# Softmax of six attention units on ScalarE, regrouped dilated units, weights decoded in two parts, and a new written order in a fused attention and two-layer MLP kernel

## The chip, the cores and the metric

The kernel runs on one core of a Trainium2 chip. Its engines are TensorE (PE, matrix products), VectorE (DVE), ScalarE (ACT), GpSimd (POOL) and SyncE (SP, which here only issues DMAs). The metric is the time of one execution on the device in microseconds (us), as the median of several runs.

## The reference

Three stages run one after the other, all in fp32.

```python
# 1 attention: q, k, v are 2 x 8 x 576 x 64
rel = pos[:, None] - pos[None, :]
mask_plain = (rel >= 0) & (rel < 32)                       # heads 0-3
mask_dil = (rel >= 0) & (rel < 128) & (rel % 4 == 0)       # heads 4-7
scores = where(mask, q @ k.T / 8, -1e9)
x = softmax(scores) @ v                  # rearranged to 1152 tokens x 512
# 2 a SoLU layer: w_in 512 x 1024, w_out 1024 x 512 (both fp64 in HBM here)
h = x @ w_in;  solu = h * softmax(h)
x = ((solu - mean) / sqrt(var + 1e-6) * g_ln) @ w_out
# 3 four experts, weighted: w1 4 x 512 x 1024, w2 4 x 1024 x 512
out = sum_e p[:, e] * (relu(x @ w1[e]) @ w2[e])
```

## The kernel before, in words

**Precision.** Every large product is made of three fp32r products: each operand is split into a rounded high part and the rest (`xhi`, `xlo`, `whi`, `wlo`), and high x high, high x low and low x high are added in PSUM. `w_in` and `w_out` come as 64-bit floats and are decoded by `convert` (L182): ACT turns the low word into a number (L186) and takes the absolute value of the high word (L188), DVE shifts it (L190) and puts the sign back (L192), and DVE or POOL adds the low part (L194). Then `conv_in` rounds the result to `whi` (L219) and subtracts to get `wlo` (L221).

**Attention** (`att_U`, L253) is done in twelve units: for each of two batches three plain units (P.0 to P.2, four heads each, 192 positions) and three dilated ones (D.0 to D.2, each four heads, two residues at a time, 96 positions of one dilated sequence of 288). A unit is a mask product and 24 QK products (L262, L271), a row maximum (L279), a subtraction (L281) and a sum (L286) on DVE, one exponential on ACT (L284), a reciprocal, a scaling (L290), a transposition on PE (L309) or by DVE and a trip through HBM (the units in `ASWAP`, L295 to L303), the product with v (AV, L320), and the split into `xhi`, `xlo`. A PSUM tile for attention comes from a pool of two. v of a plain unit comes from a pool of two buffers (`vp`, L152).

**SoLU layer.** `moe_H(t)` (L344) makes 24 products (L350) for one tile of 128 tokens, six for each of four blocks of 128 rows of `w_in`; blocks 0 and 1 take the plain heads, 2 and 3 the dilated heads. Then come maximum (L355), exponential (L357), product with h (L359) and normalisation (L362 on ACT or L364 on DVE). `moe_T` (L369) transposes the tile, for tiles 3 to 8 through HBM (`swap_T`, L391). `moe_X(c, dp)` (L421) is the product with `w_out` for a chunk of three tiles, 48 products (L432), copied out at L435.

**Experts.** `up` (L548) and `down` (L601) run from about 150 us on, with products at L545 and L617. Steps of groups g = 1 to 7 are set by loops at the end of the kernel.

**What sets the order.** Up to the first expert group the order is a list written by hand (`ORDER`, L28): each name stands for one step of a generator, up to its next `yield`, for a load (`lP`, `lD`, `lI`, `lO`, `lvp`, `lvd`) or for warm-up products on a dummy tile (`F.n`, L84). A `+` after a name sets `alt`, which gives that step's copies to DVE rather than ACT and its additions to POOL rather than DVE. Each engine, and SP for all loads, runs its instructions in that order.

Of the kernel before, what the change touches and what calls it, by code (L numbers as in the profile page):

```python
# [8 lines left out]
F32 = mybir.dt.float32  # L9
BF16 = mybir.dt.bfloat16  # L10
# [43 lines left out]
def fused_kernel(ctx, tc, qkp, qkd, vp, vd, w_in, w_out, gp, w1, w2, out):  # L54
# [50 lines left out]
    ap2 = at.enter_context(tc.tile_pool(name="ap2", bufs=2))  # L105
    early = ExitStack()
# [3 lines left out]
    for b, p in enumerate((erp, ap1)):  # L110
        qkP.append([p.tile([128, 832], F32, name=f"qkP{b}{t}", tag=f"qkP{b}{t}") for t in range(3)])
        qkD.append([p.tile([128, 896], F32, name=f"qkD{b}{t}", tag=f"qkD{b}{t}") for t in range(3)])
        vdt.append([p.tile([128, 3, 4, D], F32, name=f"vd{b}{c}", tag=f"vd{b}{c}") for c in range(3)])
# [25 lines left out]
    for r in range(1, 4):  # L139
        nc.vector.tensor_copy(mask[32 * r:32 * r + 32, 2], m0[:, 2])  # L140
# [203 lines left out]
    def moe_H(t):  # L344
        pm = psm.tile([128, 2, 512], F32, name="pm", tag="pm")
        cols = slice(128 * t, 128 * t + 128)
        for n_, kk in enumerate(KORD):
# [4 lines left out]
            if n_ % HCUT[t] == HCUT[t] - 1:  # L352
                yield
# [433 lines left out]
```

## Time and profile before

| | us |
|---|---|
| median of 3 runs (lowest, highest) | 529.58 (528.38, 531.33) |
| profiled execution, first to last instruction | 528.5 |
| PE busy | 515.0 |
| DVE busy | 356.9 |
| ACT busy | 191.7 |
| POOL busy | 187.3 |

The profile gives for each engine its busy time; a matmul counts as busy while it waits in the pipeline, so the start times of matmuls say more than their durations. Its views are a table of stretches (busy time of each engine, granted clock of PE as a share of 2.4 GHz, share and rate of the DMAs), a timeline of instructions with what ended the idle time before them, and the chain of waits, followed back from the last instruction. The span is 528.5 us and lies inside the range of the timed runs.

### The profile page before, as it was taken

Reading aid. Unit: us, or ns where it says so; the run is one execution under the profiler, and the core shown is the slowest. Engines: PE = TensorE matmul, PEld = TensorE weight load, DVE = VectorE, ACT = ScalarE, POOL = GpSimd, SP = SyncE. Lnnn points to the kernel's source line nnn. Section 1 sums busy time; section 2 is a strip of 40 time slices with the busy share of each in tenths; the row PEclk is TensorE's granted clock in tenths of the full one; section 3 lists DMA queues with packets and bytes.
Section 4 is the critical chain, followed back from the end, with each engine's and each line's share of the span. In section 5 each row is a group of like instructions: output and inputs, shape, how many; then the busy total and the mean of one; then the engine's idle time right before and its main releaser. Section 6 shows DMA issues by size and latency. Waiting matters only on the chain.

```text
span 528.5 us, 9419 instructions
## 1 busy us (share of the span) xinstructions
PE 515.0 (97%) x3971; PEld 459.0 (87%) x3971; DVE 356.9 (68%) x474; ACT 191.7 (36%) x295; POOL 187.3 (35%) x130
## 2 busy tenths in 40 slices
PE   7799999999999999999999999999999999999997
PEld 3578898888999998998989899898989889898986
DVE  6889996777978874854685485568448656853632
ACT  3768965423254432321422232142214213312210
POOL 2554220312233532730571173048117313820300
PEclk9799999999999999999999999999999999999999
DMA  8966752448043001300400040040004002000022
GB/s 311 364 239 211 242 175 97 112 141 211 16 159 141 19 2 35 126 1 1 159 1 1 0 160 0 1 141 20 2 0 161 1 0 81 0 1 1 1 81 99
DMA packets 24490, 46.44 MB, mean 88 GB/s; under 512 B 4480, under 2 KB 9088, under 8 KB 24064
## 3 DMA queue, kind: packets, MB, share of 16 engines
q1 hardware_dynamic: 24448, 45.84, 25.6%
q8 instruction: 31, 0.51, 0.4%
q14 instruction: 11, 0.09, 0.0%
HBM read 39.34 MB, written 6.49 MB: 87 GB/s over the span
## 4 chain that ended last, share of the span: by engine, by line
PE 87%; DMA 7%; DVE 4%; ACT 1%; SPq 1%; issue 0%; DVEq 0%; ACTq 0%
PE pa L617 19%; PE pm L617 18%; PE pm L545 17%; PE pa L545 17%; PE pm L350 7%; PE pm L432 6%; DMA vp<-in_vp_dram 2%; PE pa L320 2%; DMA et<-dt 2%; DMA draw<-in_moe_w_in_dram 1%; DMA dt<-st 1%; PE pa L271 1%; DVE e L359 1%; DVE e L364 1%; PE pa L381 1%; DVE st L397 0%
## 5 line engine op out<-in xcount | busy, mean ns | idle before, releaser
L558 DVE SCALAR_TENSOR_TENSOR hl<-ct,hh 128x512 fp32r<-128x512 f32 (+1 forms) x64 | 63.6, 1012 | 35.3 <-ACT hh L556 35.3
L556 ACT ACTIVATE hh<-ct 128x512 fp32r<-128x512 f32 (+1 forms) x64 | 42.1, 682 | 48.7 <-DVE ct L588 20.7
L617 PE MATMUL pa<-wl,hh 128*128 128x512 f32 (+1 forms) x148 | 57.3, 387 | 0.0
L617 PE MATMUL pa<-wh,hh 128*128 128x512 f32 (+1 forms) x148 | 57.3, 387 | 0.0
L617 PE MATMUL pa<-wh,hl 128*128 128x512 f32 (+1 forms) x148 | 57.1, 386 | 0.0
L545 PE MATMUL pm<-xoh,hl 128*128 128x256 f32 (+1 forms) x192 | 56.8, 296 | 0.0
L545 PE MATMUL pa<-xoh,hl 128*128 128x256 f32 (+1 forms) x192 | 56.8, 296 | 0.0
L545 PE MATMUL pm<-xol,hh 128*128 128x256 f32 (+1 forms) x192 | 56.8, 296 | 0.0
L545 PE MATMUL pa<-xol,hh 128*128 128x256 f32 (+1 forms) x192 | 56.8, 296 | 0.0
L545 PE MATMUL pm<-xoh,hh 128*128 128x256 f32 (+1 forms) x192 | 56.8, 296 | 0.0
L545 PE MATMUL pa<-xoh,hh 128*128 128x256 f32 (+1 forms) x192 | 56.8, 296 | 0.0
L617 PE MATMUL pm<-wl,hh 128*128 128x512 f32 (+1 forms) x144 | 55.7, 387 | 0.0
L617 PE MATMUL pm<-wh,hh 128*128 128x512 f32 (+1 forms) x144 | 55.7, 387 | 0.0
L617 PE MATMUL pm<-wh,hl 128*128 128x512 f32 (+1 forms) x144 | 55.6, 386 | 0.0
L464 POOL TENSOR_TENSOR wl<-wl,wh 128x1024 fp32r<-128x1024 f32 x7 | 16.9, 2414 | 95.3 <-ACT wh L172 95.3
L622 DVE SCALAR_TENSOR_TENSOR xf<-pm,pr,xf 128x512 f32<-128x512 f32 (+1 forms) x32 | 23.6, 738 | 31.1 <-PE pm L617 31.1
L464 POOL TENSOR_TENSOR hl<-sw,hh 128x512 fp32r<-128x512 f32 x22 | 33.5, 1522 | 30.3 <-ACT hh L172 27.6
L622 DVE SCALAR_TENSOR_TENSOR xf<-pa,pr,xf 128x512 f32<-128x512 f32 (+1 forms) x32 | 23.6, 738 | 30.3 <-PE pa L617 30.3
L172 ACT CAST wh<-wl 128x1024 fp32r<-128x1024 f32 x16 | 16.8, 1052 | 71.0 <-PE pa L617 40.5
L572 POOL TENSOR_TENSOR ct<-ct,ct 128x512 f32<-128x512 f32 (+1 forms) x15 | 21.4, 1426 | 48.1 <-ACT ct L570 42.9
L545 PEld LDWEIGHTS pm<-xoh,hh 128*128 128x128 f32 x192 | 36.4, 190 | 0.3
L545 PEld LDWEIGHTS pm<-xol,hh 128*128 128x128 f32 x192 | 36.4, 190 | 0.3
(199 smaller groups left out, 1258.9 us busy)
## 6 DMA issues: line engine op xcount, KB each, us to landing
wl<-in_moe_w_dram SPq DMA_DIRECT2D x16, 512.0 KB, 3.7
cvr<-in_moe_w_out_dram SPq DMA_DIRECT2D x8, 512.0 KB, 3.6
rw<-in_moe_w_dram SPq DMA_DIRECT2D x8, 512.0 KB, 6.0
wh<-in_moe_w_dram SPq DMA_DIRECT2D x8, 512.0 KB
draw<-in_moe_w_in_dram SPq DMA_DIRECT2D x3, 1024.0 KB, 12.8
qkD<-in_qkd_dram SPq DMA_DIRECT2D x6, 448.0 KB, 6.4
dt<-st SPq DMA_DIRECT2D x5, 512.0 KB, 3.3
et<-dt SPq DMA_DIRECT2D x10, 256.0 KB, 4.2
```

The lines of the kernel that those rows point to most:

```text
L172: nc.scalar.copy(out, in_)
L271: nc.tensor.matmul(ps[32 * g:32 * g + 32, j, 64 * m:64 * m + 64], lhsT=qt[rows, h, xq:xq + 32], rhs=kt[rows, h, xq:xq + 64], start=False, ...
L320: nc.tensor.matmul(po[64 * (g % 2):64 * (g % 2) + 64, j, o:o + 32], lhsT=vt[rows, m, g, :], rhs=pt[rows, m, g, :], start=True, stop=True)
L350: nc.tensor.matmul(pm[:, n, :], lhsT=xx[:, kk, cols], rhs=ww["in", kk][:, 512 * n:512 * n + 512], start=(n_ == 0 and i < 2), stop=(n_ == K ...
L432: nc.tensor.matmul(pm[:, dd, 0:CW], lhsT=w_, rhs=x_[:, f, :], start=(f == 0 and i == 0), stop=(f == KF - 1 and i == 2))
L464: pick().tensor_tensor(out=out, in0=a, in1=b, op=op)
L545: nc.tensor.matmul(ps[:, ff, 0:n], lhsT=a[:, kk, fc], rhs=b[:, kk, :], start=kk == 0 and m == 0, stop=kk == 1 and m == 2)
L556: nc.scalar.activation(out=hv, in_=src, func=AF.Relu)
L558: nc.vector.scalar_tensor_tensor(out=lv, in0=src, scalar=0.0, in1=hv.bitcast(F32), op0=ALU.max, op1=ALU.subtract)
L572: poolv().tensor_tensor(out=c12, in0=c21, in1=c22, op=ALU.add)
L617: nc.tensor.matmul(po[:, 0, 0:dn], lhsT=h_[:, f, cols], rhs=w_, start=(f == 0 and i == 0), stop=(f == 3 and i == 2))
L622: nc.vector.scalar_tensor_tensor(out=acc[:, t, dc], in0=po[:, 0, 0:dn], scalar=pr[:, t, e:e + 1], in1=acc[:, t, dc], op0=ALU.mult, op1=ALU ...
```

## The change

1. In the six units of batch 1 (`EXPB`), ACT makes the subtraction and the sum with the exponential: one small copy scales the six negated maxima, then six exponentials of 64 columns each read the scores from PSUM with that maximum as their bias and write the sum through the accumulator. DVE keeps the maximum and adds 1e-9 to the sums.
2. A dilated unit holds other blocks of 32 positions (`DBLK`): unit 0 has positions 0, 128 and 160, unit 1 has 32, 64 and 192, unit 2 has 224, 256 and 96. Tile 0 of the SoLU layer then needs dilated unit 0 alone. The host lays out q, k and v accordingly, and a `qkd` load is 128x1024 in place of 128x896. The write of `xhi`, `xlo` of a dilated unit has up to three pieces in place of one or two.
3. `w_in` is decoded in two parts: `conv_high` makes `whi` from the high word alone, `conv_low` adds the low word and makes `wlo`, later. They have three buffers (`evas`) in place of two.
4. Tiles 0 and 1 (`FINE`) do the products with `whi` of blocks 0 and 1 first, then those with `wlo`, then the same for blocks 2 and 3.
5. v of the plain units has three buffers; masks are three in place of four; the program is built with `dynamic_dma_scratch_size=2048`.
6. `ORDER` is new throughout, up to the first expert group.

```diff
+EXPB = ("UD.0.1","UD.1.1","UD.2.1","UP.0.1","UP.1.1","UP.2.1")
+FINE = (0, 1)
+DBLK = ((0, 128, 160), (32, 64, 192), (224, 256, 96))
 ORDER = """
-lP.0.0+ F.10 UP.0.0 UP.0.0+ lI.0 UP.0.0 lD.0.0 VI.0 VI.0 VI.0+ ...
+F.3 lD.1.0+ lP.0.0+ F.1 UP.0.0 lI.0 UP.0.0+ UP.0.0 lP.1.0+ UD.1.0 ...
...
-        t = ap2.tile([128, 3, 4, D], F32, name="vp", tag="vp")
+        t = ap3.tile([128, 3, 4, D], F32, name="vp", tag="vp")
...
+    evas = [erp.tile([128, 1024], F32, name=f"eva{i}", tag=f"eva{i}") for i in range(3)]
+    def decode_high(high, a, out):
+        au = a.bitcast(U32)
+        nc.scalar.activation(out=a, in_=high.bitcast(F32), func=AF.Abs, scale=2.0 ** -112)
+        yield
+        nc.vector.tensor_scalar(out=au, in0=au, scalar1=3, scalar2=None, op0=ALU.logical_shift_left)
+        yield
+        nc.vector.scalar_tensor_tensor(out=out.bitcast(U32), in0=high.bitcast(U32), scalar=0x80000000, in1=au, op0=ALU.bitwise_and, op1=ALU.bitwise_or)
+        yield
+
+    def decode_low(low, a):
+        au = a.bitcast(U32)
         nc.scalar.activation(out=low, in_=low.bitcast(U32), func=AF.Copy, scale=2.0 ** -29)
...
+    def conv_high(j):
+        j, sl, low, high, a = half_in(j)
...
+        yield from decode_high(high, a, a)
+        copy(whi["in", j][:, sl], a)
+
+    def conv_low(j):
+        j, sl, low, high, a = half_in(j)
+        yield from decode_low(low, a)
+        pick().tensor_tensor(out=wlo["in", j][:, sl], in0=a, in1=whi["in", j][:, sl].bitcast(F32), op=ALU.subtract)
...
+        if f"U{quad}.{t}.{b}" in EXPB:
+            nc.vector.tensor_reduce(out=st[:, 0].rearrange("p (j c) -> p j c", j=2), in_=sv, axis=AX.X, op=ALU.max)
+            yield
+            nc.scalar.activation(out=st[:, 1], in_=st[:, 0], func=AF.Copy, scale=-SCALE)
+            for i in range(3):
+                nc.scalar.activation(out=sm[:, i], in_=sv[:, 0, i], func=AF.Exp, bias=st[:, 1, i:i + 1], scale=SCALE, accum_out=st[:, 2, i:i + 1])
+            yield
...
+            nc.vector.tensor_scalar(out=st[:, 2], in0=st[:, 2], scalar1=1e-9, scalar2=None, op0=ALU.add)
+            yield
...
-        for n_, kk in enumerate(KORD):
-            seq = [(xhi, whi, n) for n in range(2)] + [(xhi, wlo, n) for n in range(2)] + [(xlo, whi, n) for n in range(2)]
...
+        parts = [(kk, p) for kk in KORD for p in ("h", "x", "l")]
+        if t in FINE:
+            parts = [(kk, p) for ks in ((0, 1), (2, 3)) for ps in (("h", "x"), ("l",)) for kk in ks for p in ps]
```

The order shows the change at three places. The first is SP's queue of loads at the start, before; `vp` is v of a plain unit (three of them, unit by unit), `vd` v of a dilated one (vd_114 of D.1, vd_113 of D.0), `draw` a block of `w_in` (draw_202 block 0 in two halves, then blocks 1, 2 and 3), `qkD` and `qkP` q and k.

```order
L147 DMA qkP_107<-in_qkp_dram 128x832
L208 DMA draw_202<-in_moe_w_in_dram 128x512
L147 DMA qkD_110<-in_qkd_dram 128x896
L205 DMA draw_202<-in_moe_w_in_dram 128x512
L147 DMA qkD_111<-in_qkd_dram 128x896
L147 DMA qkP_108<-in_qkp_dram 128x832
L147 DMA qkD_112<-in_qkd_dram 128x896
L147 DMA qkP_109<-in_qkp_dram 128x832
L208 DMA draw_394<-in_moe_w_in_dram 128x1024
L150 DMA vd_114<-in_vd_dram 128x768
L208 DMA draw_455<-in_moe_w_in_dram 128x1024
L155 DMA vp<-in_vp_dram 128x768
```

The same queue of the changed kernel, from its sixth load down to v of D.0 (vd_116); before it stand qkD of D.1, qkP of P.0, half of block 0, qkP of P.1 and qkD of D.0; vd_117 is v of D.1, qkD_122 is q and k of D.0 of batch 1, draw_200, 270, 417 and 559 are blocks 0 to 3.

```order
L209 DMA draw_200<-in_moe_w_in_dram 128x512
L209 DMA draw_270<-in_moe_w_in_dram 128x1024
L158 DMA vp<-in_vp_dram 128x768
L150 DMA qkP_112<-in_qkp_dram 128x832
L150 DMA qkD_115<-in_qkd_dram 128x1024
L153 DMA vd_117<-in_vd_dram 128x768
L209 DMA draw_417<-in_moe_w_in_dram 128x1024
L231 DMA cvr<-in_moe_w_out_dram 128x512
L158 DMA vp<-in_vp_dram 128x768
L209 DMA draw_559<-in_moe_w_in_dram 128x1024
L150 DMA qkD_122<-in_qkd_dram 128x1024
L153 DMA vd_116<-in_vd_dram 128x768
```

The first plain v and block 1 moved up; block 3 and v of D.0 moved down, behind a first piece of `w_out` (cvr) and a load of batch 1.

The second place is PE at the first products of the SoLU layer, before; wh_206 and wl_207 are the two parts of block 0 of `w_in`, wh_397 and wl_398 those of block 1, and the rows with wh_206 that come second belong to tile 1.

```order
L320 MATMUL pa<-pt,vd_114 64x32 x24
L320 MATMUL pa<-pt,vp 64x32 x24
L84 LDWEIGHTS warm
L84 MATMUL pm<-warm 128x512
L84 LDWEIGHTS warm
L84 MATMUL pm<-warm 128x512
L84 LDWEIGHTS warm
L84 MATMUL pm<-warm 128x512
L350 MATMUL pm<-wh_206,xhi 128x512 x2
L350 MATMUL pm<-wl_207,xhi 128x512 x2
L350 MATMUL pm<-wh_206,xlo 128x512 x2
```

The changed kernel from the same first products on; wh_276 and wl_277 are block 0, wh_384 and wl_385 block 1, qkD_122 is D.0 of batch 1, and the last two rows are tile 1.

```order
L388 MATMUL pm<-wl_277,xhi 128x512 x2
L388 MATMUL pm<-wl_385,xhi 128x512 x2
L275 LDWEIGHTS identb
L275 MATMUL pa<-mask,identb 128x192
L275 LDWEIGHTS identb
L275 MATMUL pa<-mask,identb 128x192
L285 MATMUL pa<-qkD_122 32x64 x24
L347 MATMUL pa<-pt,vd_116 64x32 x24
L388 MATMUL pm<-wh_276,xhi 128x512 x2
L388 MATMUL pm<-wh_276,xlo 128x512 x2
```

Products with `wl` now come apart from those with `wh`, and QK of batch 1 and AV of D.0 stand between tile 0's blocks 0, 1 and tile 1.

The third place is ACT in the softmax of batch 1, before, at a unit whose scores are in sm_129.

```order
L383 ACTIVATE e,esq<-e 128x1024
L172 CAST hh<-pa 128x8x128
L284 ACTIVATE sm_129<-sm_129 128x6x64
L383 ACTIVATE e,esq<-e 128x1024
L172 CAST hh<-pa 128x8x128
```

The changed kernel at the units with sm_131 and sm_133.

```order
L175 CAST wh_567<-eva_164 128x1024
L296 ACTIVATE st<-st 128x6
L298 ACTIVATE sm_131,st<-pa,st 128x64 x3
L301 ACTIVATE sm_131,st<-pa,st 128x64 x3
L296 ACTIVATE st<-st 128x6
L298 ACTIVATE sm_133,st<-pa,st 128x64 x3
L301 ACTIVATE sm_133,st<-pa,st 128x64 x3
L237 ACTIVATE cvr<-cvr 128x512
```

One exponential became a small copy and six exponentials that read PSUM.

## Rows read from the trace of the kernel before

**Rows 1.** Stretches: us, PE, PEld, DVE, ACT, POOL busy (count), PE clock, DMA share, GB/s

```profile
26.40:43.50 17.10, 16.80 (x348) 13.26 (x348) 15.49 (x26) 11.68 (x19) 9.62 (x6) 1.00 0.57 200
43.50:92.30 48.80, 47.60 (x686) 40.91 (x685) 43.22 (x76) 37.01 (x60) 10.17 (x9) 1.00 0.57 191
112.80:149.70 36.90, 34.30 (x195) 33.50 (x195) 30.64 (x42) 10.57 (x17) 11.10 (x7) 1.00 0.40 108
149.70:528.50 378.80, 375.52 (x2220) 341.71 (x2219) 231.66 (x265) 110.53 (x168) 139.97 (x87) 1.00 0.14 48
```

**Rows 2.** Chain of waits, 0 to 160 us: start us, us, what

```profile
9.37 12.75 DMA vp<-in_vp_dram
...
49.09 0.18 PE pa L262 x2
49.27 0.65 PE pa L271 x45
...
54.58 2.73 PE pm L350 x12
...
58.15 0.83 PE pa L320 x48
```

**Rows 3.** Timeline of ACT, PE and SP: start us, us, instruction, idle before and releaser

```profile
9.38 0.68 ACT L186 ACTIVATE draw<-draw 128x512 int32<-128x512 uint32 x1 [1.10 <-DMA draw<-in_moe_w_in_dram]
...
14.12 9.87 SPq L155 DMA_DIRECT2D vp<-in_vp_dram  x2
...
22.25 1.38 PE L320 MATMUL pa<-pt,vp 64*64 64x32 f32 x48 [0.65 <-DMA vp<-in_vp_dram]
...
24.46 1.42 PE L350 MATMUL pm<-wh,xhi 128*128 128x512 f32 x2
...
43.49 0.82 PE L309 MATMUL pa<-ident,pd 128*128 128x128 f32 x6
```

**Rows 4.** Stretches of 2 us at the start, columns as in rows 1

```profile
16.00:18.00 2.00, 2.00 (x54) 1.47 (x55) 1.93 (x5) 0.79 (x2) 2.00 (x2) 0.50 1.02 421
20.00:22.00 2.00, 0.90 (x48) 0.79 (x48) 1.97 (x3) 1.84 (x4) 0.01 (x1) 1.00 1.00 410
```

**Rows 5.** Timeline of PE, 84 to 165 us, where it waits

```profile
86.67 0.73 PE L350 MATMUL pm<-wh,xhi 128*128 128x512 f32 x2 [0.92 <-ACT xf L172]
...
92.24 0.33 PE L432 MATMUL pm<-hh,wh 128*128 128x384 f32 x1
...
96.43 0.62 PE L350 MATMUL pm<-wh,xhi 128*128 128x512 f32 x2
...
114.02 0.44 PE L432 MATMUL pm<-hl,wh 128*128 128x384 f32 x1 [0.82 <-POOL hl L419]
...
131.75 0.41 PE L432 MATMUL pm<-hh,wh 128*128 128x384 f32 x1 [0.98 <-ACT xf L172]
132.96 0.44 PE L432 MATMUL pm<-hl,wh 128*128 128x384 f32 x1 [0.80 <-DVE hl L419]
```

**Rows 6.** Timeline of DVE, the last tile's chain

```profile
115.73 1.19 DVE L355 TENSOR_REDUCE nmx<-pm 128x1 f32<-128x1024 f32 x1
...
131.68 1.23 DVE L419 TENSOR_TENSOR hl<-et,hh 128x1024 fp32r<-128x1024 f32 x1
```

**Rows 7.** Stretch from tile 0's maximum to the first late transposition, columns as in rows 1

```profile
41.00:84.50 43.50, 43.22 (x600) 37.12 (x600) 42.24 (x77) 34.28 (x56) 12.38 (x12) 1.00 0.60 195
```

**Rows 8.** Groups of instructions, 0 to 160 us: line, engine, operation, shapes, count, busy us, mean ns

```profile
L357 ACT ACTIVATE e<-pm,nmx 128x1024 f32<-128x1024 f32 x9 | 10.1, 1117 | 19.5 <-DVE nmx L355 19.5
...
L281 DVE TENSOR_TENSOR sm<-pa,st 128x384 f32<-128x384 f32 x12 | 6.7, 558 | 0.3
...
L286 DVE TENSOR_REDUCE st<-sm 128x6 f32<-128x390 f32 x12 | 6.5, 551 | 0.0
...
L284 ACT ACTIVATE sm<-sm 128x384 f32<-128x384 f32 x12 | 6.3, 524 | 6.0 <-DVE sm L281 6.0
...
L357 ACT ACTIVATION_READ_ACCUMULATOR e<-pm,nmx 128x1 f32 x9 | 1.7, 192 | 0.0
```

More of the change, by code (lines that the diff above doesn't have):

```diff
@@ L51 @@
+u.1+ u.1 WP.1
 """
@@ L111, in fused_kernel @@
         qkP.append([p.tile([128, 832], F32, name=f"qkP{b}{t}", tag=f"qkP{b}{t}") for t in range(3)])
-        qkD.append([p.tile([128, 896], F32, name=f"qkD{b}{t}", tag=f"qkD{b}{t}") for t in range(3)])
+        qkD.append([p.tile([128, 1024], F32, name=f"qkD{b}{t}", tag=f"qkD{b}{t}") for t in range(3)])
         vdt.append([p.tile([128, 3, 4, D], F32, name=f"vd{b}{c}", tag=f"vd{b}{c}") for c in range(3)])
@@ L119, in fused_kernel @@
         nc.vector.memset(sm[:, :, 64:65], 1e-9)
-    mask = ap1.tile([128, 4, 3, 64], BF16, name="mask", tag="mask")
+    mask = ap1.tile([128, 3, 3, 64], BF16, name="mask", tag="mask")
     m0 = mask[0:32]
@@ L215, in conv_in @@
             wlo["in", j] = wp.tile([128, 1024], F32R, name=f"wl{j}", tag=f"wl{j}")
-        a = (erp.tile([128, 1024], F32, name="eva", tag="eva") if j % 2 else cva)[:, sl]
-        yield from convert(dins[j][:, 2 * sl.start:2 * sl.stop], a)
-        hi, lo = whi["in", j][:, sl], wlo["in", j][:, sl]
-        copy(hi, a)
-        yield
-        pick().tensor_tensor(out=lo, in0=a, in1=hi.bitcast(F32), op=ALU.subtract)
+        yield from decode_high(high, a, a)
[4 more added lines that the diff above has]
+        pick().tensor_tensor(out=wlo["in", j][:, sl], in0=a, in1=whi["in", j][:, sl].bitcast(F32), op=ALU.subtract)
     def load_out(j, t):
@@ L228, in conv_out @@
         a = cva[:, sl]
-        yield from convert(cvr[:, 1024 * t:1024 * t + 1024], a)
+        low, high = (cvr[:, 1024 * t:1024 * t + 1024].rearrange("p (n two) -> p two n", two=2)[:, i] for i in range(2))
+        nc.scalar.activation(out=low, in_=low.bitcast(U32), func=AF.Copy, scale=2.0 ** -29)
+        yield
+        yield from decode_high(high, a, a)
+        pick().tensor_tensor(out=a.bitcast(U32), in0=a.bitcast(U32), in1=low.bitcast(U32), op=ALU.add)
+        yield
         if ("out", j) not in whi:
@@ L346, in moe_H @@
         cols = slice(128 * t, 128 * t + 128)
-        for n_, kk in enumerate(KORD):
-            seq = [(xhi, whi, n) for n in range(2)] + [(xhi, wlo, n) for n in range(2)] + [(xlo, whi, n) for n in range(2)]
-            for i, (xx, ww, n) in enumerate(seq):
+        parts = [(kk, p) for kk in KORD for p in ("h", "x", "l")]
+        if t in FINE:
+            parts = [(kk, p) for ks in ((0, 1), (2, 3)) for ps in (("h", "x"), ("l",)) for kk in ks for p in ps]
+        done = 0
+        for n_, (kk, p) in enumerate(parts):
+            xx, ww = {"h": (xhi, whi), "x": (xlo, whi), "l": (xhi, wlo)}[p]
+            for n in range(2):
                 nc.tensor.matmul(pm[:, n, :], lhsT=xx[:, kk, cols], rhs=ww["in", kk][:, 512 * n:512 * n + 512],
-                                 start=(n_ == 0 and i < 2), stop=(n_ == KD - 1 and i >= 4))
-            if n_ % HCUT[t] == HCUT[t] - 1:
+                                 start=n_ == 0, stop=n_ == len(parts) - 1)
+            if t in FINE and p != "h" or t not in FINE and p == "l" and kk % HCUT[t] == HCUT[t] - 1:
                 yield
@@ L755, in _lay_out @@
     vd = halo(v[:, 4:].reshape(b, 4, s // 4, 2, 2, n).transpose(0, 1, 4, 3, 2, 5).reshape(b, 4, 2, s // 2, n), 3)
-    vd = [[vd[:, :, :, 96 * c + 32 * m:96 * c + 32 * m + 64] for m in range(3)] for c in range(3)]
+    vd = [[vd[:, :, :, x:x + 64] for x in u] for u in DB]
     d["vd"] = _np.array(vd).transpose(2, 0, 4, 5, 1, 3, 6).reshape(b, 3, 128, -1)
```

143 lines of the change are left out of this document (77 added, 66 removed).

## The prediction

> **What bounds the kernel now.** I read the table of stretches first [rows 1]. From 149.7 us to the end, 378.8 us, PE is busy for 375.5 us: the experts are bound by PE's products, and the change touches only the first steps there. What is open lies ahead of 149.7 us. I cut that part where the tail of the first two SoLU tiles ends, at 43.49 us, where PE starts its next transposition [rows 3].
>
> Up to 43.5 us the loads decide. PE waits until 22.25 us for v of the first plain unit, and SP sits from 14.1 to 24.0 us on the third such load, for which there is no free buffer [rows 3]; in the chain of waits that v stands alone with 12.75 us, the longest piece [rows 2]. The first SoLU product starts at 24.46 us [rows 3]. The DMAs move 410 to 421 GB/s at that time and their share is full [rows 4], so it is the order of the loads, and not their number in flight, that can be bettered there.
>
> From 43.5 to 92.3 us PE is busy for 47.6 of 48.8 us, and DVE for 43.2 [rows 1]. Between the first tile's maximum and the first late transposition DVE is busy for 42.24 of 43.5 us, ACT for 34.28 [rows 7]: DVE runs level with PE, ACT has 9 us to spare.
>
> From 92 to 149.7 us PE is bound by its own work but for three late waits [rows 5]: 0.92 us at 86.67 for a copy out of PSUM; 114.02, where the second product of the second chunk of X waits 0.82 us for a low part on POOL, some 1.0 us lost with the slow start; and 131.75 to 132.96, where X's last chunk waits for the last tile's hh and then its hl. Before that wait X ran at 4.19 us for 24 products (92.24 to 96.43), so 96 from 114.0 end near 130.8, and some 2.1 us are lost there. That makes 4.0 us in all.
>
> **The change, step by step.** I sum against the profiled execution, span 528.5 us; the median of the runs is 1.1 us above it, and I add that at the end.
>
> *Loads at the start.* Sizes follow from the shapes: 128x1024 fp32 is 512 KiB, 128x832 is 416, 128x896 is 448, 128x768 is 384, a block of w_in 1024. Before, the second half of block 0 closes 1888 KiB and is used at 9.38 us; the first plain v closes 6432 KiB and is used at 22.25 us [rows 3]. That is 353 KiB per us, and I place the new loads on that line. Five loads of 2368 KiB stand ahead of those the order shows. The first plain v then closes 4288 KiB and lands at 16.2 us, 6 us sooner; v of D.1 closes 5600 (19.9 us), the second plain v 7520 (25.4), q and k of D.0 of batch 1 9056 (29.7), v of D.0 9440 (30.8 us; on the same line before: 7840 KiB, 26.2 us). With three buffers SP no longer sits on the third v.
>
> *PE up to the end of tiles 0 and 1.* Durations: QK with its mask 0.18 + 0.65 = 0.83 us, AV 0.83 us, twelve SoLU products 2.73 us, so 0.23 each [rows 2]. After v of D.1 (19.9) the first products with wh can start near 23 us, since 14 warm-up products and QK stand in the queue ahead; before it was 24.46. But PE cannot run on: AV of P.1 has to wait for 25.4, the four low products of blocks 0 and 1 end near 27.3, and then QK of D.0 of batch 1 stands in the queue and waits for 29.7, AV of D.0 right behind it for 30.8 us. From there: AV to 31.6; tile 1's ten products with blocks 0 and 1, 2.3, to 33.9; QK 34.8; tile 0's blocks 2 and 3 and the rest of tile 1 are 12 + 14 products, 5.9 us, with two QK, 1.7, a transposition of a third of a us and up to 1 us of waiting for the low part of D.0 from DVE. That ends at 42.7 to 43.7; I take 43.0, against 43.49: **-0.5 us**. By then PE has done one QK more and one AV fewer than before; both cost 0.83 us, so nothing is owed. Bounds: were all loads at the 410 KB per us that the DMAs move [rows 4], v of D.0 would land near 28.7 us, 2 us sooner (-2.5); and DVE, busy for 15.5 of the 17.1 us before 43.5 [rows 1], now also adds the low words of three whole blocks where one and a half were on it before; one or two such adds and their queue late make +3.
>
> The granted clock of PE was 0.50 at 16 to 18 us [rows 4], the lower of its two levels (1.2 GHz), after short bursts and waits; the 14 warm-up products fill such a hole. Loads, not PE, set the times above, so I cost this at nothing; if the clock were low at 31 to 43 us, 36 products at twice 0.23 us would cost 8 us more, but PE works without a break there.
>
> *Softmax of batch 1.* DVE loses six subtractions of 558 ns and six sums of 551 ns, 6.7 us [rows 8], and gets six additions of six columns, some 0.2 us each (my estimate): -5.5 us, five sixths of it in the stretch of rows 7, where DVE then has 37.7 of 43.5 us. ACT loses 524 ns per unit and gets seven instructions. The price of an exponential of 64 columns is not in the trace. Below: 64/384 of 524 ns, 87 ns. Above: a whole 384-column one and a read of the accumulator after it, 524 + 192 = 716 ns. From the slope of 524 ns at 384 and 1117 at 1024 columns (0.93 ns a column) 64 columns take 228 ns, with the read 420 ns if nothing overlaps; successive instructions on ACT do overlap, so I take 300. A unit then costs 6 x 0.30 + 0.15 = 1.95 us in place of 0.52; bounds 0.6 and 4.4. In the stretch of rows 7 five of the six units lie: 34.28 + 5 x 1.43 = 41.4 of 43.5 us.
>
> The Trainium skill (ScalarE: Activation LUTs, section What ACT_TABLE_LOAD costs) says that an ACTIVATE with a pointer as bias takes 280 ns + 0.833 ns a column, and that successive ones overlap by 93 ns. For the 1024 columns of L357 that is 1133 ns, and the row has 1117 [rows 8], so the trace agrees. By it 64 columns are 333 ns, and with overlap and read a unit comes to some 2.2 us, ACT's stretch to 42.7 us.
>
> So DVE gets room and ACT loses nearly all of its own. The gain on DVE is hidden (PE was busy through that stretch with DVE full), the loss on ACT is hidden as long as it stays below 43.5 us. I take **0** here, bounds -1.2 (PE's own slack in 43.5 to 92.3 [rows 1]) and +10.3 (ACT at 34.28 + 5 x 3.9 = 53.8 us, less the stretch).
>
> *The late waits.* Tile 5's products now come while 72 of the 96 products of X's first chunk are still to do, in place of 24, with two AV among them: 8.4 + 1.7 = 10 us more cover for its way through HBM, so the 1.0 us at 114 us goes. The copy out of PSUM at 86.67 now has two AV, 1.7 us, between the products that it follows and its user: 0.9 us goes. The last tile: its maximum starts at 115.73 [rows 6], 2.9 us after its products end at 112.8, because DVE first normalises and transposes the tile before it; now ACT normalises that one. I give the chain 1.2 us of that back, and of the 2.1 us 0.9 stay. Late next is the same hl (131.68 before [rows 6]), behind two DMA trips that nothing shortens. **-3.1 us**, bounds 0 and -4.0.
>
> *The experts.* The products are the same, and only the order of the first operands changes; X's last chunk, 16.7 us of PE, covers them. 0, bounds -0.5 and +1.5. Masks, tile sizes and scratch: 0, since PE waits for loads there.
>
> Sum: -0.5 + 0 - 3.1 = -3.6 us. 528.5 - 3.6 = 524.9 on the span, and with 1.1 us **526.0 us**.
>
> **Rivals.** (a) *The start gains too.* If the loads keep to the moved rate and DVE keeps up, the start gives -2.5 in place of -0.5: 524.0. For it: the DMAs moved 410 KB/us in full slices and SP is no longer held. Against: the loads ahead of v of D.0 grew by 1600 KiB. (b) *New small waits eat it.* DVE, ACT and PE are each near full from 41 to 84 us; where one unit's chain runs through all three, each hand-over can add some tenths. Twelve units and five tiles at 0.2 us are 3.4 us: 529.4, no change. For it: DVE at 97% lost PE 1.2 us before. Against: DVE has more room than it had. (c) *ACT becomes the bound, slower.* It decides from 43.5 us of ACT in the stretch, that is above 2.4 us a unit (0.37 us an exponential). At the unoverlapped 0.42 plus 0.15, 2.67 us a unit, ACT has 45.0 us; at 716 ns 53.8. Midway, 49.4, it is 5.9 us late: 529.6 + 5.9 - 3.6 + 1 for tiles that arrive late at X = 532.9. For it: the skill's figure is close to the limit and the reading from PSUM is untried here; against: such instructions follow one another without a gap on ACT. (d) *The low parts are late*: tile 0 ends 3 us later, the waits still go: 529.5, counted with (b).
>
> **How the numbers follow.** Forecast 0.45, own range 524.3 to 528.3; (a) 0.17; (b) with (d) 0.25; (c) 0.13. Differences under 0.5% (2.6 us, so 526.9 to 532.2) cannot be told from no change. Of the forecast two thirds lie under 526.9: faster 0.30 + 0.17 + 0.05 of (b) = 0.52; same 0.15 + 0.20 = 0.35; slower 0.13. The range takes in (a) with 2 us to spare and the nearer half of (c): 522.0 to 532.5.
>
> **What would show it.** Right: the first plain v used by 17 us; tiles 0 and 1 done between 41 and 44 us; ACT's exponentials of 64 columns near 0.3 us from start to start; DVE's busy time from tile 0's maximum to the first late transposition down by some 4 to 5 us; no wait above 0.5 us of PE at the start of X's second chunk and at most 1 us at the third; experts 379 us long. Wrong: tiles 0 and 1 done after 45 us, ACT busy throughout 41 to 84 us with PE waiting on it, or the last chunk of X starting more than 2 us after the second ends.

## The result and the profile after

The changed kernel takes 533.71 us (median of 7 runs, 531.88 to 535.61) against 529.58 (7 runs too, 528.38 to 531.33): a ratio of 1.006, interval 1.0031 to 1.0089. It is slower by more than the measurement is uncertain, and 526.0 us had been predicted. The profiled execution has a span of 531.9 us, 3.4 more than before.

I cut the span at the same two events as in the prediction: the end of tiles 0 and 1 (the next transposition on PE) and the first product of the experts. The first stretch ended at 43.49 us [rows 3] and ends at 47.47: +4.0. The second went from there to 149.54 us and goes to 152.23: 104.8 us in place of 106.0, -1.3. The experts take 379.7 us in place of 379.0, +0.7. The sum is +3.4.

PE's timeline of the changed kernel around the first v products, to be laid beside [rows 3]:

```profile
18.25 0.90 PE L347 MATMUL pa<-pt,vp 64*64 64x32 f32 x48
...
19.35 0.73 PE L285 MATMUL pa<-qkP 64*32 64x64 f32 x48
20.00 0.82 PE L87 MATMUL pm<-warm 128*128 128x512 bf16 x3
20.87 0.50 PE L347 MATMUL pa<-pt,vd 64*64 64x32 f32 x19
23.93 1.07 PE L347 MATMUL pa<-pt,vd 64*64 64x32 f32 x29 [2.56 <-issue]
```

The first plain v is used 4 us sooner, at 18.25 us in place of 22.25; the prediction had it by 17. But after 19 of the 48 products of D.1's v PE stands for 2.56 us, and the releaser is "issue": no semaphore, no engine and no load that the trace shows. Stretches of 2 us there (columns as in rows 1, answering [rows 4]):

```profile
20.00:22.00 2.00, 1.33 (x28) 0.63 (x22) 1.82 (x5) 1.37 (x2) 2.00 (x3) 1.00 1.10 436
22.00:24.00 2.00, 0.07 (x4) 0.07 (x6) 1.14 (x2) 0.73 (x1) 2.00 (x2) 0.95 0.97 395
24.00:26.00 2.00, 2.00 (x32) 1.74 (x33) 0.95 (x3) 1.85 (x3) 2.00 (x2) 0.50 0.99 400
26.00:28.00 2.00, 2.00 (x53) 1.18 (x51) 0.67 (x2) 0.00 (x0) 0.94 (x1) 0.50 1.04 402
28.00:30.00 2.00, 2.00 (x22) 1.64 (x8) 1.61 (x4) 0.40 (x1) 0.00 (x0) 0.50 1.01 392
```

PE's clock was full until the hole and stands at 0.50 (1.2 GHz) behind it, over 24 to 30 us, where PE is busy without a break and each pair of SoLU products takes 0.9 to 1.0 us in place of 0.45. The DMAs are full throughout. The same stretches of the kernel before show a lull at 24 to 28 us and a full clock from 26:

```profile
24.00:26.00 2.00, 2.00 (x6) 1.42 (x5) 1.78 (x3) 1.62 (x3) 0.60 (x1) 0.53 0.65 212
26.00:28.00 2.00, 1.70 (x22) 1.28 (x24) 2.00 (x3) 0.72 (x2) 1.17 (x1) 1.00 0.74 247
28.00:30.00 2.00, 2.00 (x99) 1.88 (x95) 0.72 (x3) 2.00 (x4) 2.00 (x1) 1.00 0.85 294
```

Yet both profiles have 6.8 us at 1.2 GHz up to there. Before has two stretches of it, the changed kernel one; here they are in full, two lines of before and one of after:

```profile
15.63:19.05 3.42, 3.13 (x56) 2.03 (x57) 2.92 (x7) 1.88 (x3) 2.79 (x3) 0.50 1.01 408
22.46:25.87 3.41, 3.41 (x54) 2.52 (x47) 3.04 (x7) 2.85 (x4) 2.14 (x1) 0.50 0.70 245
23.78:30.61 6.83, 6.68 (x91) 4.94 (x92) 3.83 (x9) 3.08 (x6) 3.16 (x2) 0.50 1.02 400
```

What differs is the work in them. Of before's 6.8 us 2.9 are warm-up products and waits, of the changed kernel's next to nothing. From the first SoLU product (24.46 us before, 24.93 after) to the end of tiles 0 and 1 PE takes 19.0 us before and 22.5 after, and 1.4 and 5.7 us of these are at 1.2 GHz. At half the rate that is 0.7 and 2.8 us lost, so I put 2.1 of the 3.5 us down to the clock (an estimate). One unit's products more stand in that part (0.83 us), and some 0.6 us are left.

What fills the hole stands in the DMA view of 21.4 to 21.6 us (queue, kind: packets, MB, share of 16 engines):

```profile
q1 hardware_dynamic: 24, 0.08, 101.2%
q8 instruction: 1, 0.02, 33.4%
```

One 16 KB packet of instructions starts there, just after PE stopped at 21.38, and takes 0.334 x 16 x 0.2 = 1.07 us; PE goes on 1.35 us after its end. The whole kernel has 31 such packets, and PE 3971 products with as many weight loads: 256 instructions a packet. So I count back from the stop (an inference: the trace doesn't name the border): the 256 instructions that ran out there began at 16.02 us, and PE used them up in 5.4 us. The next packet started 5.5 us behind that border and PE could go on 7.9 us behind it, 2.5 us too late. Before, PE took 6.8 us over the same block (14.15 to 20.98 us); its next packet started 3.9 us behind the border and was ready 6.3 us behind it, so there is no hole. The DMAs were equally full both times (416 and 418 GB/s while the packet was out). Why it came later in the changed kernel stands in no trace.

Late in the second stretch, PE's waits (what waited <- for what: us in total, times, longest) and VectorE's queue, answering [rows 5]:

```profile
PE pm L470 <- DVE xf L173: 2.3, 1, 2.3
...
PE pm L470 <- POOL hl L457: 0.7, 1, 0.7
```

```profile
90.79 1.25 DVE L435 STREAM_TRANSPOSE st<-e 128x1024 f32<-128x1024 f32 x1 [4.17 <-PE pa L347]
91.96 0.92 DVE L173 COPY xf<-pm 128x768 f32<-128x768 f32 x1
```

The four waits of before (0.92, 0.82, 0.98 and 0.80 us, 3.5 in all) have become two of 3.0 us. The two for the last tile are gone. The copy out of PSUM costs 2.30 in place of 0.92: it stands on VectorE behind tile 4's transposition, which itself waits for the last product with v. And tile 5's low part, through GpSimd, is late at X.1 again.

A unit's six exponentials on ScalarE, at 35.32 us and on:

```profile
34.97 0.26 ACT L296 ACTIVATE st<-st 128x6 f32<-128x6 f32 x1
35.32 0.32 ACT L298 ACTIVATE sm<-pa,st 128x64 f32<-128x64 f32 x1
35.53 0.19 ACT L298 ACTIVATION_READ_ACCUMULATOR sm<-pa,st 128x1 f32 x1
35.62 0.31 ACT L298 ACTIVATE sm<-pa,st 128x64 f32<-128x64 f32 x1
...
37.06 0.42 ACT L175 CAST xhi<-pa 128x128 fp32r<-128x128 f32 x1
```

They follow at 0.29 us, and the unit takes 2.1 us.

### The profile page after: what moved, and what is told of

Its sections match the earlier page's. It is cut to its first block, busy times and chain, and to the rows that moved or that the text cites. A ratio compares the mean times of both kernels' runs of the same rounds, so it can differ in the third digit from the quotient of the medians.

```text
span 531.9 us, 9504 instructions
## 1 busy us (share of the span) xinstructions
PE 517.3 (97%) x3971; PEld 459.5 (86%) x3971; DVE 350.6 (66%) x473; ACT 193.1 (36%) x362; POOL 200.6 (38%) x141
## 4 chain that ended last, share of the span: by engine, by line
PE 80%; DVE 7%; DMA 5%; ACT 3%; issue 2%; POOL 2%; SPq 0%; POOLq 0%; DVEq 0%; ACTq 0%
PE pa L655 19%; PE pm L655 18%; PE pa L583 16%; PE pm L583 16%; PE pm L388 5%; PE pm L470 3%; DMA dt<-st 3%; PE pa L347 2%; DMA qkP<-in_qkp_dram 1%; DVE xol L502 1%; PE pa L285 1%; ACT sm L298 1%; ACT sm L301 1%; DMA et<-dt 1%; PE pa L419 1%
## 5 line engine op out<-in xcount | busy, mean ns | idle before, releaser
L502 POOL TENSOR_TENSOR hl<-sw,hh 128x512 fp32r<-128x512 f32 x20 | 30.5, 1524 | 24.6 <-ACT hh L175 24.0
L583 PEld LDWEIGHTS pa<-xoh,hh 128*128 128x128 f32 x192 | 36.4, 190 | 0.8 <-issue 0.3
```

Source lines behind the costliest of these rows:

```text
L502: pick().tensor_tensor(out=out, in0=a, in1=b, op=op)
L583: nc.tensor.matmul(ps[:, ff, 0:n], lhsT=a[:, kk, fc], rhs=b[:, kk, :], start=kk == 0 and m == 0, stop=kk == 1 and m == 2)
```

## The experiments

Four theories. **A**: PE's instructions come late beside full DMAs, and hole and low clock are the loss. **B**: ScalarE's exponentials make the start late. **C**: something else stops PE at that v product. **D**: work that PE needs stands on VectorE behind waiting transpositions. Differences from the changed kernel are differences of the ratios to before, times 530 us; an interval of a ratio is about 0.003 to either side, so such a difference is uncertain by 1.9 to 2.7 us. No run undoes the new blocks of the dilated units, the decoding in two parts, the order of products in tiles 0 and 1, or the masks and the scratch size by themselves. Parts of the order are named as in the program.

**pad64.**
```diff
-F.3 lD.1.0+ lP.0.0+ F.1 UP.0.0
+F.3 lD.1.0+ lP.0.0+ F.1 N.64 UP.0.0     # N: 128x32x32 products, 2 instructions each
```


> The changed kernel with 64 very small warm-up products more (128 instructions, 32 columns each, none of the work changed) in TensorE's idle time before its first scores. Theory A (late instructions): TensorE's instructions arrive in pieces of 16 KiB, 256 instructions; the piece that was needed at 21.38 us started only at 21.51 us beside full DMAs, and the hole of 2.56 us and the low granted clock of 24 to 31 us came from that. Then 128 instructions more shift the border between pieces 128 instructions to the front of the program: the hole in the v product of D.1 is gone, the clock stays at 1.0 in 24 to 31 us, and the time falls by 1.5 to 3 us, to 531 to 532.2. Theory B (the start is late because of ScalarE's exponentials of batch 1 between 32 and 50 us): the hole may go, but tiles 0 and 1 still end near 47 us and the time stays within 0.5 us of 533.7. Theory C (something the trace does not show, such as a transfer, stops TensorE at this product): the hole stays at the same product.

Ratio 1.0076 (1.0047 to 1.0105): no gain. The hole in D.1's v product is gone, but two others came, and the clock was low again:

```profile
25.41 0.41 PE L289 MATMUL pa<-qkD 64*32 64x64 f32 x19 [1.11 <-issue]
...
33.41 0.43 PE L289 MATMUL pa<-qkD 64*32 64x64 f32 x5 [2.90 <-issue]
```

Every product has one weight load, and all of these are recorded: 349 stand ahead of the changed kernel's hole, 477 and 604 ahead of these two. That is 128 and 255 more, or 256 and 510 instructions. Each hole ends 1.3 to 1.4 us after an instruction packet. So A's mechanism holds and C falls, but the time did not fall as A forecast: moving the border only moved the hole. (The profile is of the longest of its nine executions; five of the nine had a higher mean clock, 0.997 in place of 0.987.)

**pad16.** The same with N.16.

> The changed kernel with 16 very small warm-up products (32 instructions) ahead of its first scores. Theory A (late instructions, borders every 256 instructions; a piece starts 3.2 to 5.5 us after TensorE crosses the border before it, takes 1.1 us, and TensorE goes on 1.35 us behind it): the border before is crossed at 13.6 us in place of 16.2, so its piece is ready at 19.2 to 21.5 us and TensorE needs it at 20.9: the hole in the v product of D.1 shrinks from 2.56 to 0 to 0.7 us. Two borders on, at the 1214th recorded instruction, which is now in the v product of D.0 of batch 0 (before: in the middle of long products), TensorE arrives at about 32 us and the piece is ready at 34.6 to 36.9: a hole of 2.5 to 4.8 us there. Time within 1 us of the changed kernel's 533.7. Theory C (a transfer or something else at this product): hole of 2.5 us at the v product of D.1 as before, none in that of D.0.

Ratio 1.0130 (1.0092 to 1.0169). It is 3.7 us longer where a time within 1 us was expected. At the first border (13.3 us) the hole did not shrink, since the packet started at 21.2 us, 7.9 us after it. The second hole came where it was expected, in D.0's v product, and each stands one border from the other (349 and 603 weight loads):

```profile
23.55 0.67 PE L351 MATMUL pa<-pt,vd 64*64 64x32 f32 x32 [2.57 <-issue]
...
36.03 0.43 PE L351 MATMUL pa<-pt,vd 64*64 64x32 f32 x5 [2.52 <-issue]
```

In the eight kernels with the same loads in the same order (the changed one, pad16, qklate, vp2, noexp, copyfirst, fixtail, tail2) the second packet starts after 7.1 to 7.5 MB of loads had been started, whether PE crossed the border at 13.3 us (pad16) or at 16.6 (vp2); pad64 crossed at 11.9 and had it at 15.9, after 5.1 MB. A place among the queued loads fits that better than a fixed delay, but when the packet is asked for stands in no trace.

**qklate.**
```diff
-... UP.0.0[AV] UP.2.0[QK] F.3 UD.1.0+[AV] H.0+[0] UD.2.0+[QK] UP.1.0[TP] H.0+[1]
+... UP.0.0[AV] F.3 UD.1.0+[AV] H.0+[0] H.0+[1] UD.2.0+[QK] UP.2.0[QK] UP.1.0[TP]
```


> The changed kernel with the scores of D.2 and P.2 of batch 0 (2 x 98 instructions) behind the first two steps of tile 0 on TensorE, not ahead of them; their softmax follows. Theory A (late instructions): fewer instructions are used up before the v product of D.1, so it runs through without the hole, tile 0's first products start by 22.5 us in place of 24.93, and TensorE runs dry a little later, in the scores of D.2, for 1 to 2 us; the time falls by 0.5 to 2 us. Theory C: the hole stays inside the v product of D.1. Rival: P.2's softmax, now later, makes P.2's v product and with it tiles 1 and 2 late: time 0 to 2 us longer.

Ratio 1.0101 (1.0068 to 1.0134). As A says, D.1's v product ran through and tile 0 began at 20.67 us, but PE ran dry twice, 0.75 us in D.2's scores and 1.94 us in P.1's v product. The time is 2.2 us longer, at the edge of what the runs resolve, as the rival said; whether for the rival's reason was not looked at.

**shallow.**
```diff
+pc.8 lI.2+   pc.10 lO.0.0+   pc.11 lvp.1.0   pc.12 lI.3   ...   # pc.k: 4 bytes of load k's tile to DRAM, by SP
-lI.2+        lO.0.0+         lvp.1.0         lI.3         ...
```


> The changed kernel with its loads held back: ahead of 15 of the loads SP first sends 4 bytes of an earlier load's tile to a scratch, so that it waits until that load has landed; at most about 1.5 MB are then under way, in place of some 4 MB. Nothing of the work changes. Theory A1 (a piece of instructions waits behind the transfers already queued): the piece starts 1 to 2.5 us after its border in place of 3.2 to 5.5, the hole at 21.4 us is under 0.5 us, and the time falls by 1.5 to 3 us if the loads keep 400 GB/s. Theory A2 (it waits because the DMAs are busy, whatever is queued): still 3 to 5 us and the hole stays. If the shorter queue starves the DMAs (under 370 GB/s in 13 to 36 us), the loads land 1 to 3 us late and the time rises by 1 to 3 us in either case.

Ratio 1.0091 (1.0056 to 1.0126). The third and fourth packets start 3.1 and 1.5 us after their borders (3.7 and 3.2 in the changed kernel), but the second 5.1 (5.5), and the hole of D.1's v product stays at 2.25 us, as A2 says. So A1 is borne out in small part at most. At the end of tiles 0 and 1 PE was 1.6 us ahead of the changed kernel (45.87 us), though the loads moved 309 GB/s at 20 to 36 us in place of 394. It lost that behind 89 us: the wait for VectorE's copy came again, as long as in the changed kernel, and here the clock fell behind it:

```profile
89.00:91.50 2.50, 0.28 (x20) 0.17 (x12) 2.15 (x3) 0.81 (x1) 0.00 (x0) 1.00 0.00 0
91.50:95.00 3.50, 3.42 (x11) 3.45 (x12) 2.53 (x3) 1.72 (x5) 0.00 (x0) 0.51 0.41 152
```

**short.** As shallow, with three more such waits and each one load tighter (about 1 MB under way).

> The changed kernel with its loads held back still more: at most about 1 MB is under way between 8 and 25 us. Theory A1 (a piece of instructions takes its place among the loads that are queued): the second piece starts by 18.5 us in place of 21.5, the hole in the v product of D.1 is under 0.5 us, tiles 0 and 1 are done by 45 us in place of 47.47. At the end the gain is under 1 us (ratio 1.004 to 1.010), as TensorE's wait of 2.3 us at 90 us and the low clock behind it stay. Theory A2 (the DMAs are busy, whatever is queued): the second piece still starts after 20 us. If the loads starve: tiles 0 and 1 after 47 us and the ratio over 1.010.

Ratio 1.0201 (1.0166 to 1.0236): the loads starve (241 GB/s at 20 to 36 us), PE waits 6.9 us for scores' operands (3.1 in the changed kernel), and the hole is there all the same, 2.24 us.

**vp2.**
```diff
-ap3 = at.enter_context(tc.tile_pool(name="ap3", bufs=3))
+ap3 = at.enter_context(tc.tile_pool(name="ap3", bufs=2))
```


> The changed kernel with two buffers for the v of the plain units, as before, not three; order and all else as it is. The third load of such a v is issued at 24.5 us, when the first buffer has been free since 19.2 us, so at the start nothing should move. Later loads of batch 1 may wait for a v product. Expected: within 0.7 us of the changed kernel (theories A and B alike); if the third buffer is what lets the DMAs run full through 22 to 36 us (theory A3: the third buffer is what makes the instructions late), the hole at 21.4 us goes and the time falls by over 1 us.

Ratio 1.0087 (1.0053 to 1.0120), within the uncertainty of 1.006; the hole stays at 2.54 us. The third buffer shows as neither gain nor loss beyond that uncertainty.

**noexp.**
```diff
-EXPB = ("UD.0.1","UD.1.1","UD.2.1","UP.0.1","UP.1.1","UP.2.1")
+EXPB = ()
```


> The changed kernel with the list of the six units emptied, so that their subtraction and sum are on VectorE again as in the other units; order and everything else as it is. Theory B (exponentials): ScalarE's unit goes from 2.1 back to 0.5 us, TensorE's waits between 36 and 50 us go, and the time falls by 1.5 to 2.5 us. Theory A (late instructions): the hole at 21.4 us and the low clock are as they were, and the time moves by at most 0.5 us. My forecast's step on the softmax (costs nothing either way): within 0.5 us. Against it: VectorE has about 5.5 us more to do in 35 to 80 us, where it is over 90% busy; if it is the bound there the time rises by 1 to 5 us.

Ratio 1.0126 (1.0083 to 1.0168): 3.5 us longer. B falls. VectorE is fuller where it does the softmax again, and PE idles 1.2 us there (columns as in rows 1; in the changed kernel VectorE is busy for 28.75 of these 31.3 us, and PE for 31.19):

```profile
48.00:79.30 31.30, 30.13 (x419) 25.02 (x417) 30.65 (x56) 25.89 (x46) 9.78 (x10) 1.00 0.66 197
```

PE's one long wait there, 1.1 us to 50.47, is for `pt` on ScalarE, which had itself stood for 4.44 us until VectorE's subtraction came. But a full VectorE alone doesn't explain the loss: before, VectorE was as busy (30.35 us) and PE lost nothing (31.26).

**bexp.** The same two branches put into the kernel before, for `EXPB = ("UD.2.1","UP.0.1","UP.1.1","UP.2.1")`.

> The kernel before, with its own order, where four of the six units of batch 1 (D.2, P.0, P.1, P.2) take the subtraction and the sum into ScalarE's exponential; nothing else is changed. VectorE has 3.7 us less to do, ScalarE about 6 us more (2.1 in place of 0.52 us a unit). My forecast's step: nothing, ratio 0.998 to 1.002. Rival (the softmax is what the change gains by, as emptying the list cost the changed kernel about 3 us): ratio 0.994 to 0.998. Rival c (ScalarE becomes the bound): ratio 1.003 to 1.010.

Ratio 1.0143 (1.0110 to 1.0177), 7.6 us longer: rival c in that order. PE waits for ScalarE's `sm` 2.1 and 2.4 us, and is busy for 26.64 of 31.3 us at 48 to 79.3. Nearly the same edit (six units here, four there) is worth -3.5 us in one order and +7.6 in the other.

**copyfirst.**
```diff
-endA T.4 X.0.1+ X.0.0 T.4+
+endA X.0.1+ T.4 X.0.0 T.4+      # the copy of X.0, then tile 4's transposition
```


> The changed kernel with one pair of steps swapped: VectorE copies the finished products of X.0 out of PSUM before it transposes tile 4, not behind it. Theory D (a queue behind a wait): at 90.8 us the copy stood behind a transposition that waits for the last product with v; the wait of 2.3 us that TensorE had at 90.8 to 93.0 falls to about 1.1 us, and as much less is seen at the end: 0.5 to 1.2 us off. Rival (given back): tile 4's chain starts 0.9 us later, X.1 waits longer for tile 5's low part at 118 us, and the end moves by less than 0.4 us.

Ratio 1.0074 (1.0044 to 1.0105): given back. The wait at 90.8 us is gone, and a wait of 1.96 us stands at 101.34 for low parts that queue on VectorE behind tile 5's transposition, which waits for the one buffer `st`.

**fixtail.** copyfirst, and
```diff
-T.5+ UP.1.1 X.0.0+ UD.2.1 T.4 UD.2.1 H.6+     # T.5+: tile 5's transposition
+UP.1.1 X.0.0+ UD.2.1 T.4 UD.2.1 T.5+ H.6+
-H.7 H.7 T.5+ T.6 X.1.0                        # T.5+: its low part, GpSimd
+H.7 H.7 T.5 T.6 X.1.0                         # VectorE
```


> The changed kernel with three steps of VectorE's queue changed: X.0's copy ahead of tile 4's transposition, the low parts of the last two units of attention ahead of tile 5's transposition, and tile 5's low part on VectorE (about 1.1 us) in place of GpSimd (2.39 us). Theory D (work that TensorE needs stands on VectorE behind transpositions that wait for a v product or for the one buffer st): with the first swap alone the wait came back at 101.3 us behind tile 5's transposition; with all three, TensorE's 2.3 us at 90.8 and 0.7 us at 118.2 go, X.1 starts at 115.5 to 117 us in place of 118.85, and the time falls by 1.5 to 2.5 us. Rival (tile 5's chain over the DMAs sets X.1's start whatever is ahead of it): X.1 starts after 118 us, and the time moves by under 0.5 us.

Ratio 1.0111 (1.0073 to 1.0149). No late wait over 0.3 us until 116 us, and then 4.29 us for tile 5's low part: on VectorE it stood behind tile 8's transposition and a maximum, and ran at 119.50. The clock was low behind this wait too.

**tail2.** fixtail, with that low part further forward, ahead of tile 8's transposition (`T.8+`):
```diff
-T.5 H.8+ T.8+ T.6 H.7 H.7 T.5 T.6 X.1.0
+T.5 H.8+ T.5 T.8+ T.6 H.7 H.7 T.6 X.1.0
```


> The changed kernel with the three edits of the run before on VectorE's queue, and tile 5's low part now right behind its high part, ahead of tile 8's transposition. Theory D (the place in VectorE's queue): tile 5's high part is done at 115.7 us, its low part at 116.9 in place of 120.7, TensorE comes at 116.2 and waits under 1.2 us; with the 2.3 us at 90.8 gone too, the time falls by 1.5 to 2.5 us against the changed kernel (ratio to before 1.001 to 1.004). Rival (tile 5's chain over the DMAs): the low part comes after 118.5 us again, and the time moves by under 0.5 us.

Ratio 1.0018 (0.9998 to 1.0037): 2.2 us less than the changed kernel (uncertain by 1.9), as D said. X.1 starts at 115.0 us, with two waits left at its start:

```profile
115.00 0.41 PE L470 MATMUL pm<-hh,wh 128*128 128x384 f32 x1 [0.57 <-DVE e L397]
116.14 0.41 PE L470 MATMUL pm<-hl,wh 128*128 128x384 f32 x1 [0.72 <-DVE hl L457]
```

**shorttail.** short and tail2 together.

> Both edits together, the loads held back to about 1 MB and VectorE's late steps in the new order. If start and tail each cost what theories A1 and D say and neither gives back what the other brings, the time falls by 2.5 to 4.5 us against the changed kernel: ratio to before 0.997 to 1.003. If the middle of the kernel (VectorE, 48 to 80 us) sets the end whatever comes before it, the ratio is that of the tail's edit alone, within 0.001.

Ratio 1.0134 (1.0107 to 1.0162), a miss: no hole in D.1's v product, but the starved loads cost more. The second packet started 2.7 us behind its border, with the loads of short, where the hole was; so the loads alone don't fix its delay either. Against short 3.6 us are off (uncertain by 2.4): the tail's edit gains on this start too.

**shalltail.** shallow and tail2 together, the best the runs point to.

> The changed kernel with the milder holding back of the loads (about 1.5 MB under way) and VectorE's late steps in the new order (as in the run that took 2.2 us off). If the two parts of the loss are separate (the start: instructions late beside full DMAs; the tail: VectorE's queue), the start's 1.6 us that the held-back loads brought by 80 us, and that the wait at 90 us then swallowed, now reach the end: 1 to 2 us less than with the tail's edit alone, ratio to before 0.997 to 1.001. If the middle sets the end whatever the start does: 1.001 to 1.003, as with the tail's edit alone. If holding the loads back costs elsewhere: over 1.003.

Ratio 1.0023 (1.0001 to 1.0044): 3.6 us less than shallow, which confirms the tail's edit, but no less than tail2. Its profiled span, 528.1 us in place of tail2's 529.6, comes from an execution with a higher mean clock (0.999 in place of 0.994), and holes of 1.61 and 1.15 us remain. So thinner loads add nothing that the runs resolve, and no version beat the kernel before.

**btail7.** The kernel before:
```diff
-SWAP = (3, 4, 5, 6, 7, 8)
+SWAP = (3, 4, 5, 6, 8)                 # tile 7 by TensorE, between X.1.0 and X.1.1
-T.5+ H.8+ H.8 ... T.5+ X.1.0 X.1.0+ sc
+T.5+ T.5 H.8+ H.8 ... X.1.0 X.1.0+     # T.5: low part on VectorE; sc behind tile 7
```


> The kernel before with two of its late waits taken away by themselves: tile 5's low part on VectorE right behind its high part (wait of 0.82 us at 113.2 us), and tile 7 transposed by TensorE between X.1's halves in place of the way over DRAM (waits of 0.98 and 0.80 us at 130.8 and 132.2 us; TensorE has 0.9 us more work). My forecast's step on the late waits: they are on the path, so the time falls by about 0.8 + 1.8 - 0.9 = 1.7 us, ratio 0.995 to 0.999. Rival (such waits are given back in the chain to the experts): ratio 0.999 to 1.002.

Ratio 1.0028 (1.0002 to 1.0054). It is 1.5 us longer (uncertain by 1.4). The last tile's two waits went, but tile 5's of 0.82 us became 0.98, and VectorE's scales, which had to move behind tile 7, made the first expert's operands late:

```profile
151.73 0.36 PE L544 MATMUL pm<-xoh,hh 128*128 128x256 f32 x1 [2.67 <-DVE xf L169]
```

The run doesn't show whether the two waits were on the path, since a longer one came in their place.

## Why the prediction was wrong

*Loads.* Too slow a line, on the harmless side: I had the second plain v land at 25.4 us and v of D.0 at 30.8, on 353 KiB a us. The loads kept 394 to 410 GB/s from 13 to 36 us; by 27.6 us 9.9 MB had been started, and v of D.0 closes the first 9.7.

*PE up to the end of tiles 0 and 1* is the step that failed: -0.5 predicted, bounds -2.5 and +3, +4.0 measured. I took the loads and VectorE as all that could hold PE and "cost the clock at nothing". After 9.9 us PE waited for no load in this stretch. What it lacked was instructions: the new order puts P.0's v product, P.2's scores and D.1's v product next to each other, and PE went through a block of 256 instructions in 5.4 us in place of 6.8. With DMAs as full as before, the next packet started 5.5 us behind its border in place of 3.9; why later stays open. So the first SoLU product came at 24.93 us and not near 23, with a hole of 2.56 us ahead of it. pad64 and pad16 show that the stops are at 256-instruction borders and follow them. And the clock was not free: I had written that "PE works without a break there", and it did work without a break over 24 to 30.6 us, at 1.2 GHz. From the first SoLU product to the end of the stretch I had 20.0 us; it took 22.5, 5.7 of them at the low clock, which is 2.8 us by half the rate (an estimate).

That division is read from traces and not shown by a run: no run took the hole away and kept the loads as they are. The clock is not all of it either. Of the changed kernel's seven executions the two with a mean clock of 0.997 span 530.1 and 530.3 us, the five at 0.993 or 0.994 span 531.6 to 533.8. Executions of the kernel before in the other experiments have a median span of 527.7 us at 0.997 (15 of them) and of 529.0 at 0.993 or 0.994 (18), so at the same clock the changed kernel is still 2.5 to 3.2 us longer by the medians.

*Softmax.* 0 predicted, on the ground that PE hid VectorE's load. The unit cost of 1.95 us was right but for a tenth (2.1). The Trainium skill's figure (ScalarE: Activation LUTs, What ACT_TABLE_LOAD costs), which I had worked out to 2.2 us, was as near. But the term is -3.5 us in this order (noexp, uncertain by 2.7), more than the -1.2 that I had as the bound, and +7.6 for four units in the old one (bexp): what it is worth depends on the order around it, and busy shares alone don't tell it.

*The late waits.* -3.1 predicted, -0.5 measured on the waits and -1.3 on the stretch. The last tile did better than I gave it (both waits gone). Tile 5 did not gain its 1.0 us, and the copy out of PSUM got 1.4 us worse, though I counted two v products as cover: they ran behind the copy's own products, and the copy stood in VectorE's queue behind a transposition waiting for them. copyfirst to tail2 show that it is the queue: once three such places were moved, 2.2 us came back (uncertain by 1.9), and 3.6 in each of the pairs short and shorttail, shallow and shalltail.

*Experts.* 0 predicted, +0.7, within the bounds.

Of the rivals none had the mechanism. (b), 529.4, named small waits and not a hole; (c) came near the time, 532.9, for the wrong reason.

## What to carry to other kernels

Where DMAs run full, count PE's instructions as a transfer too: here tiny products used up 256 instructions in 5.4 us, faster than the next packet came, and an "issue" wait of 1 to 3 us, 256 instructions from the next such wait and ended by an instruction packet, was the mark of it. After a reordering, read each in-order queue for work that PE needs standing behind an instruction that waits; three such places, moved together, were worth 2.2 us. A cost moved between engines is only worth what the order of its neighbours makes of it, so try it with the order it will have.

## What the runs showed of the hardware

- An instruction packet of 16 KB started 0.3 and 0.8 us behind its border where the DMAs moved under 80 GB/s (the changed kernel, near 38 and 43 us), and 2.2 to 7.9 us behind it where they moved some 300 to 418; it took about 1.1 us, and PE went on 1.3 to 1.5 us after it. The Trainium skill (Runtime: NRT & Kernel Launch, Instruction fetch mechanics) says that code is fetched in blocks of 16 KiB, 256 instructions, and that the cost of crossing such a border is mostly hidden. The size agrees with the trace (31 packets for 7942 instructions); the hiding does not, by holes of up to 3.1 us (copyfirst).
- A wait of PE of 2.3 to 4.3 us was followed by a stretch at 1.2 GHz in some executions and not in others: not at 91 us in the changed kernel's profile, at 91.5 to 95 us in shallow's. The two low stretches of before came behind waits of 0.85 us at most.
- A 64-column exponential with accumulator takes 0.31 us with 0.19 for the read, and the next starts 0.29 us after it.
